# An adaLN block on one core: modulation rows folded in DRAM, half of the third block reloaded, and a new order of the last products

## The chip, the cores and the metric

The kernel runs on one core of one Trainium2 chip. The metric is the time of the whole execution on the device in microseconds (us), the median of several runs. The numbers of the profile come from one execution that was recorded by the hardware profiler; its own time stands beside the span in the table below.

## The reference, cut to what matters

```python
mod = (silu(c) @ w_mod).reshape(1, 6, 1, -1)            # c: 1 x 512, w_mod: 512 x 3072
sa, ca, ga, sb, cb, gb = (mod[:, i] for i in range(6))
h = layernorm(x) * (1 + ca) + sa                          # x: 2048 x 512
x = x + ga * linear_attention(h, wqkv, wo)                # 32 heads of 16
h = layernorm(x) * (1 + cb) + sb
x = x + gb * (mish(h @ w1 + b1) @ w2)                     # 512 -> 1792 -> 512
```

Everything is float32.

## The kernel before, in words

**Blocks and precision.** The 2048 rows are four blocks of 512 rows, numbered 0 to 3. Each float32 operand of a matmul is split into an upper part (ScalarE, a copy to `fp32r`) and a lower part (VectorE, a subtraction); a product is then three matmuls, upper by upper, upper by lower, lower by upper.

**The modulation.** `w_mod` lies transposed in DRAM (`wmodt`, 3072 x 512), and `load_wmod(i)` (L165) brings 128 of its rows into the tile `wm_i`. `mod_col(i, ...)` (L247) multiplies the tile by silu(c) and sums along the row on VectorE, which gives one column of `mc`, the table of modulation columns. Tiles 0 to 11 are plain rows. Tiles 12 to 23 (shift, scale and gate of the second half of the network) need their rows in another order, in which the 512 features are cut into pieces of 32, so `load_wmod` makes four DMAs of 32 rows each for one tile (L171, L172). All of them are issued on SP's queue. `mod_side` (L537) loads a tile and multiplies it three ticks later; tiles 20 to 23 and 16 to 19 are handled beside the query products of blocks 0 and 1 (from `beside_q`, L1026), tiles 12 to 15 beside the query product of block 2. A tick is one call of `tick()` (L121), which lets every running side job take one step; the order of instructions on each engine is thus fixed by the program's text. A product of w1's rows in the same other order is already folded by a copy from DRAM to DRAM, `fold_rows` (L806), in the loop over blocks at b == 1.

**Attention.** After the query products stand, for each block, the division by the attention's denominator (`attend`, L901: rows of 1/den are written to DRAM, read back broadcast as the tiles `rd`, and VectorE multiplies them into `q` on L925), the split into `qs` and the output product `o_unit` (L947), whose twelve matmuls per 128 rows use `qs_0` to `qs_3` in turn.

**The MLP.** Both GEMMs of the MLP use the Strassen scheme in Winograd's form: two blocks of rows are taken together, and seven products m1 to m7 replace eight. The first GEMM runs as `pair(L, g)` (L1510) for L = 0 (blocks 0, 1) and L = 2 (blocks 2, 3) and g = 0 to 6. The second GEMM consists of units (L1577), each one product for one g and both halves of 128 columns; `units` (L1869) lists them in order. For L = 2 the order is m1, m2, m4, m5, m6, m7, m3, and every product is a run of 42 matmuls of 512 columns over g = 6, 0, 1, ... 5 (`ORDER`, L1574). m6 and m7 add onto the accumulator of m1 (`pa`), m3 in effect onto m5, m2 has `pb`, m4 has `pd`, m5 has `pc`. The accumulators `pa`, `pb`, `pc` take two PSUM banks of the four with the tag `acc`; for L = 2, m4 takes banks with the tag `h`. The left operand of a unit is made by `left_job` (L1473): sums of activations for m5, m6 and m3 on VectorE (L1484, L1480, L1490 to L1493), then the split, upper part on ScalarE (L1283), lower part on VectorE (L1289). The right operand is loaded by `right_job` (L1456) from sums of w2 that were stored in DRAM (`w2d`, `w2t`).

**How results leave.** With L = 2 the left half of block 2 comes from m1 and m2. `result_job` (L1630) gates it on VectorE (L1636), transposes it (L1647) and adds it into the block's residual `x1d[2]` in DRAM by an accumulating DMA on POOL's queue (L1657). The right half of block 2 is two parts: one from m5 and m6 by the same path, one from m3. m3 is computed last and the other way round, four groups t of 128 rows of 21 short matmuls (L1930 on); its end (`ends`, L1938) multiplies by the gate and adds onto `rows_t`, whole rows of block 2 that were reloaded from `x1d[2]` after both sums had landed (L1909 to L1913). `put` (L1944) writes the whole rows to the output. Block 3 is added on chip: its residual is loaded as `rq` (L1603), `rows_half` (L1661) gates, transposes and adds m7's and m5's results in four pieces (c = 0, 1 by i = 0, 1), and after the last of them four DMAs write the block with pieces of 128 columns (L1684 to L1688). Blocks 0 and 1 are copied from `x1d` to the output inside DRAM by `copy_out` (L1716), a job that is added when the first unit of m4 of L = 2 comes up (L1901).

**Who sets the order.** From the MLP on, the order of instructions comes from a planner that runs when the kernel is built (`drive`, L1229; `best_job`, L1164): jobs carry a due time, and a model of costs in the table `T` (L27) decides which step of which job each engine's queue gets next. DMAs marked ANY go to POOL's or SP's queue, whichever the model has free; eight DMAs may be outstanding per queue (`lanes`, L1130). Each engine executes its queue in order, so an instruction that waits holds all that stand behind it.

## Time and profile before

| what | number |
|---|---|
| time, median of 3 runs | 485.88 us (485.56 to 488.79) |
| time of the profiled execution | 486.17 us |
| its span, first to last instruction | 484.4 us |
| TensorE (PE) busy | 97% of the span |
| VectorE (DVE), ScalarE (ACT), GpSimd (POOL) busy | 86%, 66%, 33% |
| mean granted TensorE clock | 0.993 |

The page and the views divide the span by engine. A row of the timeline gives start, duration, engine, line, operation, output<-inputs and shape; what stands in brackets is the idle time of the engine before it, and what ended that. PEld is TensorE's weight load, SPq, ACTq and POOLq are the queues that issue DMAs. In the table by windows, a number in brackets counts instructions, and the last three columns are the granted TensorE clock, the mean busy share of the sixteen DMA engines, and GB/s. In the table of DMA queues a row has packets, MB and the time that the packets took as a share of sixteen engines' time.

### The profile page before, as it was taken

The page shows a single profiled execution, that of the slowest core. Times are in us where ns is not written, and L with a number is a line of the kernel's source. Part 1 is how long each engine was busy: PE and PEld are TensorE (multiplying, and loading weights), DVE is VectorE, ACT ScalarE, POOL GpSimd, SP SyncE. Part 2 cuts the span into 40 slices and gives each one's busy share as a digit, 9 for nine tenths or more (in the row PEclk, how much of TensorE's full clock was granted, in tenths as well). Part 3 has the DMA queues.
Part 4 walks back from the last instruction along what each step waited for, and adds up shares of the span by engine and source line. Part 5 has one row for each costly group of instructions (what it writes and reads, how often), then busy time and mean ns, then how long its engine had stood idle before and what let it go on. Part 6 is the DMA issues. An engine that isn't in the chain of part 4 may idle for free.

```text
span 484.4 us, 7380 instructions
## 1 busy us (share of the span) xinstructions
PE 471.9 (97%) x2300; PEld 386.0 (80%) x2300; DVE 418.2 (86%) x818; ACT 322.0 (66%) x583; POOL 159.7 (33%) x239
## 2 busy tenths in 40 slices
PE   8999999999998999999999999999999999999993
PEld 6788887877886888888888888877888888888793
DVE  6989999899779878999987899989986587989892
ACT  6777686865543888779988998577567548627310
POOL 4583320000012413136543132542132243833250
PEclk9999999999998999999999999999999999999998
DMA  8953699143598456469999675986253389999977
GB/s 311 401 201 89 179 166 263 33 142 101 166 239 201 143 146 202 175 200 352 390 285 300 211 227 163 266 299 213 71 162 91 100 211 267 226 333 278 234 98 239
DMA packets 73776, 101.43 MB, mean 209 GB/s; under 512 B 24001, under 2 KB 46025, under 8 KB 73706
## 3 DMA queue, kind: packets, MB, share of 16 engines
q1 hardware_dynamic: 48104, 55.99, 36.8%
q0 software_dynamic: 24144, 43.67, 35.8%
q10 hardware_dynamic: 1490, 1.31, 0.9%
q8 instruction: 18, 0.29, 0.3%
q14 instruction: 20, 0.16, 0.1%
HBM read 69.48 MB, written 35.13 MB: 216 GB/s over the span
## 4 chain that ended last, share of the span: by engine, by line
PE 80%; DMA 6%; DVE 5%; SPq 3%; ACT 2%; issue 2%; POOL 0%; ACTq 0%; DVEq 0%
PE p_a L1506 18%; PE pa L1591 12%; PE p_s L1506 7%; PE pc L1591 6%; PE pb L1591 4%; PE o L140 3%; PE o L138 3%; PE o L139 3%; PE pq_a L475 3%; PE pd L1591 3%; DMA wm<-in_wmodt_dram 2%; SPq L333 2%; PE pk L140 2%; PE pk L138 2%; PE pk L139 2%
## 5 line engine op out<-in xcount | busy, mean ns | idle before, releaser
L1521 ACT ACTIVATE u<-p_a 128x512 f32<-128x512 f32 x42 | 24.9, 595 | 25.3 <-PE p_a L1506 23.5
L1530 ACT ACTIVATE u_a<-c_a,b1c 128x512 f32<-128x512 f32 x42 | 30.3, 722 | 16.2 <-DVE c_a L1527 14.0
L1527 DVE TENSOR_TENSOR c_a<-p_s,u 128x512 f32<-128x512 f32 x28 | 19.3, 688 | 15.7 <-PE p_s L1506 9.4
L1657 POOL DMA_DIRECT2D x1d<-turned x20 | 22.1, 1743 | 29.2 <-DVE turned L1647 29.2
L1465 POOL DMA_DIRECT2D wt_m<-w2t x25 | 20.0, 1216 | 30.0 <-PE pc L1591 8.2
L1465 POOL DMA_DIRECT2D wt_m<-w2d x17 | 13.3, 1035 | 18.6 <-DVE s_5l L1289 5.5
L1480 DVE TENSOR_TENSOR u_a<-u_a,u_a 128x512 f32<-128x512 f32 x28 | 18.1, 687 | 0.0
L913 POOL DMA_DIRECT2D rden_d<-rden x2 | 1.4, 715 | 50.3 <-DVE rden L911 50.3
L938 POOL DMA_DIRECT2D x1d<-r x16 | 9.0, 564 | 24.1 <-DVE r L942 16.8
L273 POOL TENSOR_TENSOR rs_n<-rs_n,half 128x1 f32<-128x1 f32 x16 | 11.2, 704 | 15.1 <-DVE rs_n L299 8.9
L366 ACT ACTIVATE e_k<-pk 128x512 f32<-128x512 f32 x15 | 8.9, 592 | 10.7 <-PE pk L140 10.6
L1625 ACT ACTIVATE U<-pa,mc 128x512 f32<-128x512 f32 x10 | 6.9, 687 | 11.4 <-PE pa L1591 11.2
L249 DVE SCALAR_TENSOR_TENSOR wm<-wm,sc_row 128x512 f32<-128x512 f32 x16 | 10.6, 679 | 3.4 <-DMA wm<-in_wmodt_dram 3.4
L1307 POOL DMA_DIRECT2D w1p<-w1d x12 | 9.2, 766 | 12.6 <-ACT u_a L1530 3.0
L369 DVE SCALAR_TENSOR_TENSOR ku<-e_k,relu_k 128x512 f32<-128x512 f32 x15 | 10.7, 714 | 2.9 <-ACT relu_k L367 2.9
L273 POOL TENSOR_TENSOR rs_x<-rs_x,half 128x1 f32<-128x1 f32 (+1 forms) x10 | 7.8, 781 | 16.0 <-DVE rs_x L268 14.6
L925 DVE SCALAR_TENSOR_TENSOR q<-q,rd 128x512 f32<-128x512 f32 x16 | 10.5, 687 | 2.9 <-DMA rd<-rden_d 2.9
L369 DVE SCALAR_TENSOR_TENSOR q<-e_q,relu_q 128x512 f32<-128x512 f32 x16 | 10.7, 687 | 2.6 <-ACT relu_q L367 2.6
L378 POOL DMA_DIRECT2D ku<-ku x8 | 7.1, 890 | 16.5 <-DVE ku L369 16.5
L1527 DVE TENSOR_TENSOR c_a<-p_a,u 128x512 f32<-128x512 f32 x14 | 9.6, 686 | 2.9 <-PE p_a L1506 2.2
L1558 ACT ACTIVATE u_a<-p_a,b1c 128x512 f32<-128x512 f32 x14 | 9.6, 684 | 3.0 <-PE p_a L1506 2.8
L1289 DVE TENSOR_TENSOR l_m_6l<-u_a,l_m_6h 128x512 fp32r<-128x512 f32 x12 | 8.2, 688 | 1.9 <-ACT l_m_6h L1283 1.8
(1505 smaller groups left out, 1889.3 us busy)
## 6 DMA issues: line engine op xcount, KB each, us to landing
wt_m<-w2t SPq DMA_DIRECT2D x27, 256.0 KB, 9.0
wt_m<-w2t POOLq DMA_DIRECT2D x25, 256.0 KB, 6.4
wt_m<-w2d POOLq DMA_DIRECT2D x17, 256.0 KB, 9.2
r<-in_x_dram SPq DMA_DIRECT2D x16, 256.0 KB, 2.7
x1d<-r POOLq DMA_DIRECT2D x16, 256.0 KB, 4.2
x<-in_x_dram SPq DMA_DIRECT2D x15, 256.0 KB, 5.4
w2d<-b SPq DMA_DIRECT2D x15, 256.0 KB, 8.2
w1d<-in_w_dram SPq DMA_DIRECT2D x4, 896.0 KB, 6.2
```

Of the source, the lines that this page charges most:

```text
L138: pe.matmul(o, st[0], mv[0], start=start, stop=False)
L139: pe.matmul(o, st[0], mv[1], start=False, stop=False)
L140: pe.matmul(o, st[1], mv[0], start=False, stop=stop)
L273: pool.tensor_tensor(y, y, half[:, lo:hi], op=ALU.pow)
L369: dve.scalar_tensor_tensor(dst, e, 1.0, r, op0=ALU.min, op1=ALU.add)
L1465: q.dma_start(f32(v), (w2d if src == "w2d" else w2t)[g][:, :, part, :])
L1506: pe.matmul(p, st, mv, start=onto is None and c == 0 and i == 0, stop=c == 1 and i == 2, skip_group_check=onto is not None)
L1521: act.activation(t["u", n], t["pa"], AF.Copy)
L1527: dve.tensor_tensor(t[key], t[p], t["u", n], op=ALU.add)
L1530: act.activation(u, t[key], AF.Mish, bias=b1c[:, f:f + 1])
L1591: pe.matmul(o, st[:, cs], mv, start=not onto and n == 0 and k == 0, stop=n == G - 1 and k == 2, skip_group_check=onto)
L1657: q.dma_start(rows_, sq, accum_op=ALU.add)
```

## The change

Five things are done together. (1) Twelve DMAs copy the second half of `wmodt` inside DRAM into `wmd`, already in the other order, right after w1's last fold; tiles 12 to 23 then load with one DMA each. (2) The second GEMM of L = 2 runs its products in the order m1, m2, m5, m6, m4, m7, m3. (3) Of block 2 only the right half is reloaded (`rows_t` is 128 x 4 x 64) and written at the end; the left half is copied from `x1d[2]` to the output inside DRAM, once its sum has landed. (4) Block 3 leaves in two sets of four DMAs, left halves of the strips after c = 0, right halves after c = 1, and gather, turn and addition of one piece are one step of the planner. (5) For four of the seven g of m3 the lower parts are subtracted on POOL instead of VectorE. Besides, due times and costs in `T` change, for the planner to use.

```diff
- 'early_at': -1.0,
+ 'early_at': -1.3,
- 'squares_due': 96.5,
- 'turn_due': 88.0,
+ 'squares_due': 89.9,
+ 'turn_due': 82.3,
- 'left_early': 16.4,
+ 'left_early': 17.4,
- 'copy_due': 10.8,
- 'result_due': 3.8,
+ 'copy_due': 12.9,
+ 'result_due': 3.7,
- 'out01': 48.2,
+ 'out01': 53.7,
- 'add': 0.8}
+ 'by_pool': 4,
+ 'left_out': 10.0,
+ 'add': 0.1}
...
+    wmd = drp.tile([3 * D, 512], F32, name="wmd")
+    def fold_mod(n, c):
+        sp.dma_start(wmd[D * n:D * (n + 1), :].rearrange("(x c r) f -> c r x f", c=4, r=32)[c],
+                     wmodt[D * (n + 3):D * (n + 4), :].rearrange("(c x r) f -> c r x f", c=4, r=32)[c])
     def load_wmod(i):
         wm[i] = sb(f"wm_{i}")
-        if i < 12:
-            sp.dma_start(wm[i], wmodt[P * i:P * (i + 1), :])
-        else:
-            r0 = 512 * (i // 4) + 32 * (i % 4)
-            for c in range(4):
-                sp.dma_start(wm[i][32 * c:32 * (c + 1), :], wmodt[r0 + P * c:r0 + P * c + 32, :])
+        src, r0 = (wmodt, P * i) if i < 12 else (wmd, P * (i - 12))
+        sp.dma_start(wm[i], src[r0:r0 + P, :])
...
             if b == 1:
                 fold_rows(t, sp)
+                if t == 3:
+                    for n in 2, 1, 0:
+                        for c in range(4):
+                            fold_mod(n, c)
...
+    BY_POOL = (2, 3, 4, 5)[4 - T['by_pool']:]
...
     def split_steps(...):
-            dve.tensor_tensor(lo, t, f32(hi), op=ALU.subtract)
+            (pool if lower_on == POOL else dve).tensor_tensor(lo, t, f32(hi), op=ALU.subtract)
...
-        yield d_(lower, n, makes=makes)
+        yield step_(POOL, 1.4, lower, makes=makes) if lower_on == POOL else d_(lower, n, makes=makes)
...
     def rows_half(...):
+        def chain():
+            gather()
+            turn_()
+            dve.tensor_tensor(v(), v(), t3(q[1]), op=ALU.add)
-        yield d_(gather, needs=[] if keep else [("T4", L)])
-        yield d_(turn_)
-        yield d_(lambda: dve.tensor_tensor(v(), v(), t3(q[1]), op=ALU.add), needs=[("rq", L, 1)], makes=[("v", c, i)])
-        for n in range(4) if c and i else ():
+        yield d_(chain, 1600, needs=[("rq", L, 1)] + ([] if keep else [("T4", L)]), makes=[("v", c, i)])
+        for n in range(4) if i else ():
             def put(queue, n=n):
-                sq, rows_ = strip_squares(rq[L, 1], out_rows(L + 1), n)
+                sq, rows_ = strip_squares(rq[L, 1], out_rows(L + 1), n, 64 * c, 64 * (c + 1))
                 queue.dma_start(rows_, sq)
...
-    units += [(L, name, g) for name in ("m1", "m2", "m4", "m5", "m6", "m7") for g in ORDER[L]]
+    units += [(L, name, g) for name in ("m1", "m2", "m5", "m6", "m4", "m7") for g in ORDER[L]]
...
             if l == L and (name, g) == ("m6", ORDER[L][0]):
                 add_job(load_r(L, 1), now[0] + T['r_due'])
+                add_job(iter([dma_(lambda q: q.dma_start(left_half(out_rows(L)), left_half(x1d[L])),
+                                   (), [("sum", L, 0, 0)])]), now[0] + T['left_out'])
             if l == L and (name, g) == ("m7", ORDER[L][0]):
                 def rows_in(q, i):
-                    rows01.append(sb(f"rows_{i}"))
-                    q.dma_start(rows01[i], x1d[L][P * i:P * (i + 1), :])
-                add_job(iter([dma_(lambda q, i=i: rows_in(q, i), [("rows", i)], [("sum", L, 0, 0), ("sum", L, 0, 1)])
+                    rows01.append(sb(f"rows_{i}", F32, (P, 4, 64)))
+                    q.dma_start(rows01[i], right_half(x1d[L])[P * i:P * (i + 1)])
+                add_job(iter([dma_(lambda q, i=i: rows_in(q, i), [("rows", i)], [("sum", L, 0, 1)], size=LATE / 2)
...
-                            q.dma_start(out[512 * L + P * t:512 * L + P * (t + 1), :], rows01[t])
+                            q.dma_start(right_half(out_rows(L))[P * t:P * (t + 1)], rows01[t])
```

`left_half(d)` and `right_half(d)` take columns 0 to 63 and 64 to 127 of each of the four strips of 128 columns of a row, pieces of 64 float32 numbers, 256 bytes.

More of the change, by code (lines that the diff above doesn't have):

```diff
@@ L1274, in drive, with split_steps @@
             run_job(*best_job())
-    def split_steps(name, get, keep, key, makes, needs=(), n=512, then=None):
+    def split_steps(name, get, keep, key, makes, needs=(), n=512, then=None, lower_on=DVE):
         st = []
@@ L1496, in left_job @@
         yield from split_steps(f"l_{L}_{name}_{g}", lambda: s1s[L, g] if v is None else get(v), left, (L, name, g),
-                               [("l", L, name, g)], needs)
+                               [("l", L, name, g)], needs, lower_on=POOL if L and name == "m3" and g in BY_POOL else DVE)
     def product(L, g, lft, rgt, tag="h", onto=None):
@@ L1678, in rows_half @@
         t3 = lambda t: t.rearrange("q (m s) -> q m s", s=32)
+        def chain():
+            gather()
+            turn_()
+            dve.tensor_tensor(v(), v(), t3(q[1]), op=ALU.add)
         if keep:
             yield a_(kept, makes=[("U3", L, i)])
-        yield d_(gather, needs=[] if keep else [("T4", L)])
-        yield d_(turn_)
-        yield d_(lambda: dve.tensor_tensor(v(), v(), t3(q[1]), op=ALU.add), needs=[("rq", L, 1)], makes=[("v", c, i)])
-        for n in range(4) if c and i else ():
+        yield d_(chain, 1600, needs=[("rq", L, 1)] + ([] if keep else [("T4", L)]), makes=[("v", c, i)])
+        for n in range(4) if i else ():
             def put(queue, n=n):
-                sq, rows_ = strip_squares(rq[L, 1], out_rows(L + 1), n)
+                sq, rows_ = strip_squares(rq[L, 1], out_rows(L + 1), n, 64 * c, 64 * (c + 1))
                 queue.dma_start(rows_, sq)
-            yield dma_(put, (), [("v", a, b) for a in range(2) for b in range(2)], queue=(SP, ACT)[n % 2])
+            yield dma_(put, (), [("v", c, 0), ("v", c, 1)], queue=(SP, ACT)[n % 2])
     U2, U3 = {}, {}
@@ L1717, in copy_out, with left_half, right_half @@
         q.dma_start(out_rows(b), x1d[b])
+    def left_half(d):
+        return d.rearrange("n (c s) -> n c s", c=4)[:, :, 0:64]
+    def right_half(d):
+        return d.rearrange("n (c s) -> n c s", c=4)[:, :, 64:P]
     def norm_job(b, t):
@@ L1938, in ends @@
                         def ends():
-                            v = nat(rows01[t], 1)
+                            v = rows01[t].rearrange("p c (x r) -> p x c r", r=32)
                             q = sb(f"q_last_{t}", F32, (P, H))
```

## The prediction

> **What bounds the kernel now.** I read the page first, then TensorE's rows for places where it stands still.
>
> ```profile
> span 484.4 us, 7380 instructions
> PE 471.9 (97%) x2300; PEld 386.0 (80%) x2300; DVE 418.2 (86%) x818; ACT 322.0 (66%) x583; POOL 159.7 (33%) x239
> ```
>
> PE is the bound, and the change takes no matmul away. So time can come from two places only: gaps of PE inside the span, and the stretch after PE's last matmul. The windows around the one large gap:
>
> ```profile
> 149.00:153.00 4.00, 2.37 (x8) 0.99 (x7) 4.00 (x9) 2.39 (x6) 2.14 (x4) 1.00 0.67 192
> 153.00:157.00 4.00, 3.95 (x10) 3.17 (x11) 4.00 (x9) 0.91 (x2) 0.75 (x2) 0.57 1.01 217
> ...
> 150.23 0.40 PE L140 MATMUL o<-m_1h,qs_1l 128*128 128x512 f32 x1
> 151.29 0.50 PE L138 MATMUL o<-m_2h,qs_2h 128*128 128x512 f32 x1 [0.66 <-ACT qs_2h L146]
> 153.05 0.79 PE L140 MATMUL o<-m_2h,qs_2l 128*128 128x512 f32 x1 [1.02 <-DVE qs_2l L152]
> ```
>
> PE is busy 2.37 of 4 us while VectorE is busy all 4. Three products start between 150.23 and 153.05, one of them between the last two rows; at the 0.227 us of a run of 42 in 9.52 us (quoted below) they take 0.68, so 2.1 us are lost. In the next 4 us the granted clock is 0.57, which loses 4 x 0.43 = 1.7 us. Together 3.8 us. Why is VectorE late?
>
> ```profile
> 138.35 0.69 DVE L249 SCALAR_TENSOR_TENSOR wm<-wm,sc_row 128x512 f32<-128x512 f32 x1
> 142.49 0.69 DVE L249 SCALAR_TENSOR_TENSOR wm<-wm,sc_row 128x512 f32<-128x512 f32 x1 [3.44 <-DMA wm<-in_wmodt_dram]
> 143.30 1.29 DVE L925 SCALAR_TENSOR_TENSOR q<-q,rd 128x512 f32<-128x512 f32 x2
> 149.89 1.29 DVE L925 SCALAR_TENSOR_TENSOR q<-q,rd 128x512 f32<-128x512 f32 x2
> 152.31 0.69 DVE L152 TENSOR_TENSOR qs_2l<-q,qs_2h 128x512 fp32r<-128x512 f32 x1
> ```
>
> It stood 3.44 us before a modulation tile; from there to `qs_2l` it works through its list without a pause. That tile was late on SP's queue:
>
> ```profile
> wm<-in_wmodt_dram SPq DMA_DIRECT2D x48, 64.0 KB, 3.2
> 133.00 3.20 SPq L172 DMA_DIRECT2D wm<-in_wmodt_dram  x7
> ```
>
> Seven pieces cost the queue 3.20 us, 0.46 each; one 256 KB tile is four of them.
>
> The end:
>
> ```profile
> 428.17 9.52 PE pd L1591 x42
> 456.09 0.70 ACT U L1625
> 456.83 9.82 PE pa L1591 x42
> 476.60 0.13 PE m L140
> 477.21 0.42 DVE rows L1942
> ...
> 470.02 2.23 POOL L1911 DMA_DIRECT2D rows<-x1d  x4 [3.48 <-DMA x1d<-turned]
> 476.21 0.43 DVE L1942 TENSOR_TENSOR rows<-rows,q_last 128x256 f32<-128x256 f32 x1 [1.44 <-DMA rows<-x1d]
> 468.17 0.75 DVE L1671 SCALAR_TENSOR_TENSOR q<-pa,mc,T 128x512 f32<-128x512 f32 x1
> 471.99 0.89 SPq L1687 DMA_DIRECT2D out_dram<-rq  x2
> 474.46 3.56 SPq L1945 DMA_DIRECT2D out_dram<-rows  x2
> ```
>
> PE ends at 476.7, the last addition at 477.6, the last store is issued by 478.0, and the span ends at 484.4: 7.7 us after PE, 6.4 after the issue. The queues by window show why:
>
> ```profile
> DMA  9999999999999999999999996653211100000000
> ...
> q1 hardware_dynamic: 601, 0.30, 52.4%
> q10 hardware_dynamic: 590, 0.29, 51.9%
> ```
>
> The first line is 476 to 484.4 in slices of 0.21 us: the DMA engines are full until 481.0, done by 482.7, and the wrap-up takes the last 1.7. The other two are 475.5 to 477.5, almost only 512-byte pieces of block 3: 1.043 x 16 x 2 us / 1191 = 28.0 ns a piece. The reload of `rows` and the stores of block 3 and block 2 all come within these ten microseconds.
>
> **The change part by part.**
>
> *Modulation loads.* 48 pieces become 12 DMAs, so SP is free of 36 x 0.46 = 16 us of issuing. Even if a slot of SBUF holds the tile in question until the 133.00 of the row above, its only DMA is out 0.5 us later instead of three pieces after that, 1.4 us of the 3.44 at the least; the queue's 16 us make the whole of it likely. Behind the wait the next source is `rd`:
>
> ```profile
> 134.37 1.82 POOL L917 DMA_DIRECT2D rd<-rden_d  x3 [2.74 <-PE pq L140]
> DMA to landing us min/median/max: 4.9/7.2/8.2
> ```
>
> The first lands at 134.4 + 4.9 = 139.3 at the earliest, and VectorE would ask at 143.30 - 3.44 = 139.9; the second may cost up to about 1 us. `qs_2l` then ends at 153.0 - 3.4 = 149.6 to 150.6. PE wants it three products after 150.23, at 150.9. So the gap closes, narrowly, and with it the slow clock: gain 3.8. Bounds: 0 if `rd` takes the wait's place whole, 3.8 above.
>
> *The twelve folds.* 3.1 MB inside DRAM, issued after w1's.
>
> ```profile
> w1d<-in_w_dram SPq DMA_DIRECT2D x4, 896.0 KB, 6.2
> SPq L176 <- DVE ku L369: 16.5, 1, 16.5
> 30.00:60.00 30.00, 30.00 (x150) 25.09 (x150) 26.81 (x54) 20.77 (x34) 15.24 (x23) 1.00 0.43 114
> ```
>
> Four folds of 896 KB, 3.7 MB, land in about 6 us each, overlapping; I take 8 to 12 us for the twelve. SP has 16.5 us of nothing to do right behind them and the DMA engines are at 0.43, so I cost them at 0. Without that cover the next load of wq would wait, and what is late next is `q_left`, with 40 us to go: still 0. Bounds 0 to 1.
>
> *Order of products.* m6 comes 9.5 us earlier, m4 goes between m6 and m7. The wait of m7 for U2 (456.09 to 456.83) goes: 0.3 gained. But m5 now follows m2 directly, and its two `acc` banks are m2's own, which VectorE has to gather first:
>
> ```profile
> 427.53 0.75 DVE L1636 SCALAR_TENSOR_TENSOR q<-pb,mc,U 128x512 f32<-128x512 f32 x1 [1.99 <-PE pb L1591]
> ```
>
> The first bank is free at 428.3, PE wants it at 428.17; the second is free at 429.0, or 429.6 if another subtraction stands between. Cost 0.1 to 1.4, and I take 0.4, near the low end, since PE fills the first half for 0.7 us before it needs the second. Net +0.1. The sums for m5 and m6 are needed 9.5 us earlier, m4's splits later; VectorE's 1.99 us of idle in that row says that it has room. If it has not, each us late is one us of PE, and `qs`-like waits may lower the clock again.
>
> *Block 2 in halves, sum 9.5 us earlier.* The reload of `rows` can start some 9 us before 470.02, so the 1.44 us wait at 476.21 goes, with 512 KB of loading out of the last ten us. The copy of the left half and those of blocks 0 and 1 (moved with m4) fall into the stretch of m4 and m7; I cost them at 0 behind those 19 us of matmuls, and up to 1.5 if m3's tiles queue behind them.
>
> *Four subtractions on POOL, one chain.* VectorE's gather for m7's second half starts at 468.17, though PE wrote it by 466.65: subtractions for m3 stood before it. Four of them leave, at 0.69 each. They do not come free:
>
> ```profile
> 13.66 1.30 POOL L152 TENSOR_TENSOR wk_2l<-wr,wk_2h 128x512 fp32r<-128x512 f32 x1
> 14.42 1.08 DVE L658 TENSOR_TENSOR hT_x_1l<-hf_x,hT_x_1h 128x512 fp32r<-128x512 f32 x1
> 18.84 0.68 DVE L658 TENSOR_TENSOR hT_x_3l<-hf_x,hT_x_3h 128x512 fp32r<-128x512 f32 x1
> ```
>
> One takes POOL 1.30, and a subtraction of VectorE beside POOL takes 1.08 and not 0.68. So the relief is 4 x (0.69 - 0.40) = 1.2 us. The left half of block 3 can be issued near 468.9 (gather from 466.9, turn, addition), its pieces move from about 470.8, the right half two us later.
>
> *The stores.* Block 3 is now 4096 pieces of 256 bytes, block 2's half 2048. No plain store of that size is in the trace. The nearest rows:
>
> ```profile
> q1 hardware_dynamic: 7311, 0.91, 50.0%
> q0 software_dynamic: 2123, 0.55, 90.8%
> y_x<-xd SPq DMA_DIRECT2D x16, 64.0 KB, 2.8
> ```
>
> The first is 60 to 72 us, plain 128-byte pieces: 0.5 x 16 x 12 us / 7311 = 13.1 ns. The second is 462 to 470 us, accumulating pieces of 256 bytes: 54.7 ns. On the line from 13.1 (128) to 28.0 (512), 256 bytes take 18 ns. I take 18, as plain pieces resemble plain ones: 6144 x 18 / 16 = 6.9 us from 470.8, done by 477.7, before the last store is issued. Then that store is alone: issue from 477.67, 2.8 us to land as the loads of the third row, 1.7 of wrap-up: 482.2 in place of 484.4. Gain 2.2; bounds -9.1 (54.7 ns) and 2.8.
>
> *Due times in T.* They change the planner's order only, from the MLP on.
>
> ```profile
> 157.00:445.00 288.00, 287.93 (x1336) 236.81 (x1336) 251.67 (x480) 212.58 (x386) 105.22 (x156) 1.00 0.76 220
> ```
>
> From 157 to 445 us PE is never idle, so there is nothing to gain there; the 36 us of VectorE's idle time in this row are the cover, and I cost the edits at 0. Where the cover fails, a late operand is a wait of PE; I allow up to 1.5.
>
> Sum on the profiled execution: 486.17 - 3.8 - 2.2 + 0.1 = 480.3. That execution is 0.3 above the median of the runs, so the forecast is 480.0 us.
>
> **The rivals.**
>
> *Small pieces cost as much as 512-byte ones.* At 28.0 ns the stores take 10.8 us and end at 481.6; the tail gives 1.1 and not 2.2: 481.1. For it: in the same window a piece of 512 bytes costs barely more than twice one of 128. Against it: the line through both.
>
> *Slower: each 256-byte piece is read and written back.* The place is the last 15 us. At 54.7 ns, 6144 pieces take 21.0 us from 470.8, the span ends at 493.5, and the time is 480.0 + 2.2 + 9.1 = 491.3. It decides from about 41 ns a piece, where it eats the front's gain. Against it: only accumulating pieces show that price. The Trainium skill, "DMA: Bandwidth & Descriptors", Specifications, speaks for it: transfers below 512 bytes make the DMA engine read, modify and write. The 128-byte pieces at 13.1 ns, all loads, do not bear that out; no run here shows it for stores.
>
> *The front's gap stays in part.* If `rd` or a full VectorE list makes PE wait 1 us or more there, the clock may fall again, and 1.9 to 3.8 us come back: about 483. For it: the margin above is 0.3 to 1.3 us.
>
> *A new wait near the end.* The four POOL subtractions (5.2 us) stand in POOL's queue with the reload of `rows`, whose wait for the sum was 3.48 us; m3 needs them from 467.4 on. Or m5 waits long for its banks. Price 2.5: 482.5.
>
> **How the numbers follow.** Forecast 0.51, 512-byte price 0.18, gap stays 0.13, new wait 0.12, slower 0.06. A measurement of this kernel can tell about 1%, that is 481.0 and 490.7. Below 481.0 lies most of the forecast (0.45), nearly half of the first rival and a little of the others: 0.56. Above 490.7: the slow rival and a corner of a bad planner order, 0.07. Within: 0.37. The range goes from 478.2 (all upper bounds) to 484.5 (gap and tail each half missed); only the slow rival and a sum of two bad cases lie outside.
>
> **What would show it.** Right: no wait of VectorE on `wm` near 140, clock 1.00 from 149 to 157, about 12 SP issues of 256 KB for tiles 12 to 23; PE's last matmul some 3.7 us earlier; under 6 us from there to the end; 256-byte pieces near 18 ns. Wrong: DMA engines full until the end, a wait of m5 over 1 us at m2's end, a wait of m3 on POOL, or any PE gap between 157 and 445.

## The result, and the profile after

The kernel after takes 481.53 us (median of 4 runs, 480.9 to 482.57), the kernel before 486.82 in the same comparison (4 runs, 485.56 to 488.79): a ratio of 0.9897, 95% interval 0.9863 to 0.9932. The profiled execution took 481.15 us, 5.0 less than the one of before. In a second comparison, with more runs of before, the ratio was 0.9868 (0.9831 to 0.9905). The page's head:

```profile
span 479.4 us, 7305 instructions
PE 469.4 (98%) x2300; PEld 385.0 (80%) x2300; DVE 419.7 (88%) x814; ACT 322.1 (67%) x583; POOL 164.1 (34%) x241
```

The 5.0 us can be laid out along TensorE (PE), which does the same 2300 matmuls in both kernels. The first row of each pair below is of before, the second of after (timeline, start and duration in us); the rows are the first matmul of the MLP.

```profile
202.65 0.39 PE L1506 MATMUL p_a<-b_0h,a_0h 128*128 128x512 f32 x1
```

```profile
198.63 0.39 PE L1515 MATMUL p_a<-b_0h,a_0h 128*128 128x512 f32 x1
```

So 4.0 us are won before the MLP. From there to the last block's m1 the kernel after takes 0.8 longer (207.1 against 206.3), for m1 to m7 0.6 longer (58.15 against 57.52), and from the last matmul to the end 2.4 less (5.6 against 8.0). -4.0 + 0.8 + 0.6 - 2.4 = -5.0.

**The front, after.** The DMA issues (count, KB each, median us to landing):

```profile
wmd<-in_wmodt_dram SPq DMA_DIRECT2D x12, 256.0 KB, 7.6
wm<-wmd SPq DMA_DIRECT2D x12, 256.0 KB, 6.0
```

VectorE's products with the modulation tiles among the groups (busy us, mean ns of one, idle us ahead of them), and then its only wait between 136 and 150 (us in total, times, longest):

```profile
L253 DVE SCALAR_TENSOR_TENSOR wm<-wm,sc_row 128x512 f32<-128x512 f32 x16 | 10.5, 675 | 0.0
```

```profile
DVE q L933 <- DMA rd<-rden_d: 1.3, 1, 1.3
```

The two windows in which the gap lay:

```profile
149.00:153.00 4.00, 3.83 (x17) 2.86 (x16) 4.00 (x11) 2.50 (x6) 2.09 (x4) 1.00 0.79 220
153.00:157.00 4.00, 4.00 (x46) 3.00 (x45) 4.00 (x9) 1.48 (x3) 0.97 (x2) 1.00 0.18 44
```

VectorE no longer waits for a `wm` tile (idle 0.0 in that group), and waits 1.3 for `rd` instead. PE is busy 3.83 of 4 us where it was 2.37, and the granted clock of the next window is 1.00 where it was 0.57.

**The middle, after.** A wait that before did not have, in the timeline on PE, behind it on VectorE, and the store behind both on POOL:

```profile
312.11 0.50 PE L1600 MATMUL pd<-l_m_4h,t_4l 128*128 128x512 f32 x1 [1.34 <-DVE t_4l L1298]
...
311.36 0.69 DVE L1298 TENSOR_TENSOR t_4l<-t,t_4h 128x512 fp32r<-128x512 f32 x1 [1.69 <-DMA w2t<-t_3h]
...
304.64 0.55 POOL L1456 DMA_DIRECT2D w2t<-t_3h  x1 [0.25 <-ACT t_3h L1292]
```

`t_4l` is to be written where `t_3h` still lies; the store of `t_3h` was issued at 304.64 and had not landed.

**The last products, after.** The timeline of PE where m5 (`pc`) follows m2 (`pb`), and two rows of the chain that ended last, VectorE's second gather of m2 and the product behind m5:

```profile
424.54 0.39 PE L1600 MATMUL pb<-l_m_5h,wt_m 128*128 128x512 f32 x1
425.14 0.47 PE L1600 MATMUL pc<-l_m_6h,wt_m 128*128 128x512 f32 x1 [0.21 <-issue]
...
425.67 0.40 PE L1600 MATMUL pc<-l_m_6h,wt_m 128*128 128x512 f32 x1
426.35 0.50 PE L1600 MATMUL pc<-l_m_6h,wt_m 128*128 128x512 f32 x1 [0.28 <-DVE q L1645]
...
425.55 0.76 DVE q L1645
...
435.48 9.52 PE pa L1600 x42
```

In each pair the starts lie 0.60 and 0.68 us apart, where a run has 0.23. So m5 waited twice, 0.37 and 0.45 us, until VectorE had read m2's banks (the gather at 425.55 is the second). The profile puts the first wait down to `issue`; the kernel with m5 in other banks, below, shows that both were for banks. Behind them the products follow each other without a gap.

**The end, after.** The timeline of VectorE, with the first piece of block 3 (gather, transpose, addition) and the second addition, and of GpSimd (POOL) beside it:

```profile
459.32 0.75 DVE L1680 SCALAR_TENSOR_TENSOR q<-pa,mc,T 128x512 f32<-128x512 f32 x1 [1.62 <-PE pa L1600]
460.11 0.71 DVE L1684 STREAM_TRANSPOSE t<-q 128x512 f32<-128x512 f32 x1
460.85 3.37 DVE L1691 TENSOR_TENSOR rq<-rq,t 128x512 f32<-128x512 f32 x1
465.66 0.69 DVE L1691 TENSOR_TENSOR rq<-rq,t 128x512 f32<-128x512 f32 x1
...
460.75 1.67 POOL L1298 TENSOR_TENSOR l_m_4l<-u_a,l_m_4h 128x512 fp32r<-128x512 f32 x1
462.01 1.66 POOL L1298 TENSOR_TENSOR l_m_5l<-u_a,l_m_5h 128x512 fp32r<-128x512 f32 x1
```

The DMA engines from 470 to 479.4 (40 slices of 0.235 us, then packets, MB and share per queue):

```profile
DMA  9988799998999999999999998589999721000000
DMA packets 5979, 1.48 MB, mean 158 GB/s; under 512 B 5979, under 2 KB 5979, under 8 KB 5979
q10 hardware_dynamic: 3097, 0.77, 42.9%
q1 hardware_dynamic: 2882, 0.71, 37.8%
```

The same addition takes 3.37 us beside GpSimd's subtractions and 0.69 without them. The DMA engines are full to 477.4, 3.6 us behind the start of the last matmul; nearly all packets are pieces of 256 bytes (the mean is 248), and one costs 0.807 x 16 x 9.4 us / 5979 = 20.3 ns.

### The profile page after: what moved, and what is told of

The parts are those of the page before. It is cut to its first block, busy times and chain, and to the rows that moved or that the text cites. A ratio compares the mean times of both kernels' runs of the same rounds, so it can differ in the third digit from the quotient of the medians.

```text
span 479.4 us, 7305 instructions
## 1 busy us (share of the span) xinstructions
PE 469.4 (98%) x2300; PEld 385.0 (80%) x2300; DVE 419.7 (88%) x814; ACT 322.1 (67%) x583; POOL 164.1 (34%) x241
## 4 chain that ended last, share of the span: by engine, by line
PE 80%; DVE 9%; DMA 4%; issue 2%; SPq 2%; ACT 1%; POOL 1%; ACTq 0%; DVEq 0%; POOLq 0%
PE p_a L1515 18%; PE pa L1600 12%; PE p_s L1515 7%; PE pc L1600 6%; PE pb L1600 4%; PE o L142 3%; PE o L140 3%; PE o L141 3%; PE pq_a L479 3%; PE pd L1600 3%; PE pk L142 2%; SPq L337 2%; PE pk L140 2%; PE pk L141 2%; PE gacc L141 1%
## 5 line engine op out<-in xcount | busy, mean ns | idle before, releaser
L1474 POOL DMA_DIRECT2D wt_m<-w2t x29 | 24.1, 1179 | 43.4 <-PE pa L1600 16.8
L1292 ACT ACTIVATE l_m_6h<-u_a 128x512 fp32r<-128x512 f32 x12 | 7.4, 621 | 6.1 <-DVE u_a L1489 6.1
```

The costliest lines, as they stand in the source:

```text
L1474: q.dma_start(f32(v), (w2d if src == "w2d" else w2t)[g][:, :, part, :])
```

## The experiments

In the table, "front" is the start of the MLP's first matmul, "middle" from there to the last block's m1, "products" from m1 to m3, and "tail" from the start of the last matmul to the end of the span, all in us of the one profiled execution. The time is the median; the ratio is to the kernel before, run in turns on the same chip (its median was 488.18 beside the fold alone, the kernel without it, the subtractions on VectorE and the old order; 488.31 beside after again, the old due times and the two kernels with whole stores and rows; 487.23 beside the last four of the table). Runs of before are far apart (484.7 to 490.1), so a ratio is less sharp than the kernel's own runs. The tail repeats better: five executions share the order, the stores and the place of the subtractions (after twice, without fold, old due times, old `add`), and their tails lie between 5.6 and 5.9.

| kernel | time | ratio, 95% interval | front | middle | products | tail |
|---|---|---|---|---|---|---|
| before | 486.82 | 1 | 202.65 | 206.3 | 57.5 | 8.0 |
| after | 481.53 | 0.9897 (0.9863 to 0.9932) | 198.63 | 207.1 | 58.15 | 5.6 |
| after, again | 481.33 | 0.9868 (0.9831 to 0.9905) | 200.32 | 206.5 | 58.2 | 5.8 |
| fold alone | 483.40 | 0.9898 (0.9875 to 0.9920) | 199.40 | 206.2 | 57.5 | 9.0 |
| without fold | 485.99 | 0.9962 (0.9939 to 0.9986) | 203.96 | 208.2 | 58.2 | 5.7 |
| subtractions on VectorE | 480.62 | 0.9843 (0.9819 to 0.9867) | 199.89 | 206.8 | 58.2 | 4.7 |
| old order | 483.53 | 0.9890 (0.9861 to 0.9919) | 199.14 | 206.8 | 59.0 | 7.3 |
| old due times | 481.02 | 0.9858 (0.9820 to 0.9896) | 200.62 | 206.65 | 58.2 | 5.8 |
| block 3 stored whole | 483.01 | 0.9898 (0.9859 to 0.9938) | 199.54 | 206.5 | 58.2 | 7.8 |
| whole rows of block 2 | 482.89 | 0.9900 (0.9864 to 0.9935) | 198.00 | 206.9 | 58.2 | 6.8 |
| VectorE and banks | 479.64 | 0.9851 (0.9830 to 0.9872) | 198.95 | 206.4 | 57.1 | 4.7 |
| old `add` | 482.19 | 0.9898 (0.9882 to 0.9913) | 199.91 | 206.6 | 58.2 | 5.9 |
| VectorE, banks, old `add` | 479.78 | 0.9850 (0.9827 to 0.9873) | 199.23 | 206.8 | 57.1 | 5.0 |
| old order, VectorE | 481.93 | 0.9890 (0.9871 to 0.9908) | 198.36 | 209.4 | 57.55 | 5.7 |

The theory at the outset: the fold closes the front's gap and that is most of the gain; the tail's gain is made by the early sums and the earlier stores, less what GpSimd's subtractions cost. The rival: the parts depend on each other, or other edits (due times, order) made the gain.

### The fold alone

Before, with `wmd`, `fold_mod` and the new `load_wmod`, and nothing else.

> The kernel before with one part of the change: the twelve folding transfers in DRAM and the single loads of 256 KB for the last twelve modulation tiles. Nothing else is changed. Theory (the fold alone closes the front gap): TensorE's first qkv product group ends about 3.7 us earlier, VectorE waits for no `wm` near 140, the clock granted in 149 to 157 is 1.00, and the time is the time of before less 3.3 to 4.1, so about 482.4 profiled against 486.17. Rival (the front gap closed because of the other due times, or the gain in the front is given back in the planned middle): 484.5 to 486.2.

Measured: 483.40 against 488.18, 4.8 less by the medians. The profiled 483.77 lies between the two expectations (about 482.4, and 484.5 or more). The front comes 3.25 earlier in the one profile. In the windows there the clock stays at 1.00 as in after, while PE is busy for 3.07 us of the first and not for 3.83:

```profile
149.00:153.00 4.00, 3.07 (x14) 2.15 (x13) 4.00 (x9) 3.24 (x7) 2.48 (x5) 1.00 0.71 180
153.00:157.00 4.00, 4.00 (x46) 3.05 (x45) 4.00 (x10) 0.71 (x2) 0.07 (x1) 1.00 0.37 84
```

The waits:

```profile
PE o L140 <- DVE qs_2l L152: 0.9, 1, 0.9
DVE q L931 <- DMA rd<-rden_d: 2.0, 2, 1.2
```

The fold is the cause of the gain in the front. It is not complete: VectorE now waits 2.0 us for `rd`, and PE 0.9 for `qs_2l`, but the clock stays at 1.00. The tail, 9.0, gained nothing without the other parts; it was 1.0 longer than in the profile of before.

### After without the fold

```diff
...
-        src, r0 = (wmodt, P * i) if i < 12 else (wmd, P * (i - 12))
-        sp.dma_start(wm[i], src[r0:r0 + P, :])
+        if i < 12:
+            sp.dma_start(wm[i], wmodt[P * i:P * (i + 1), :])
+        else:
+            r0 = 512 * (i // 4) + 32 * (i % 4)
+            for c in range(4):
+                sp.dma_start(wm[i][32 * c:32 * (c + 1), :], wmodt[r0 + P * c:r0 + P * c + 32, :])
...
-                if t == 3:
-                    for n in 2, 1, 0:
-                        for c in range(4):
-                            fold_mod(n, c)
```

The tensor `wmd` and `fold_mod` are gone, too.

> The kernel after with the fold taken back alone: the twelve folding transfers are gone and the last twelve modulation tiles come by four pieces each again. Everything behind the front stays. Theory: the front gap is back (TensorE's wait at 149 to 153, granted clock under 0.8 in 153 to 157), the tail keeps its gain, and the time is 481.15 + 3.7 = 484.8 profiled, that is 1.3 us under before. Rival (the two parts are not independent: the gain in the tail hangs on the earlier arrival): 486 or more.

Measured: 485.99 against 488.18, 2.2 less by the medians, and a tail of 5.7 that kept its gain. By the time alone the rival's "486 or more" came true (the median is at its edge, the profiled execution took 487.75), but before itself was slower beside these runs (488.18), and the tail kept its gain without the fold. Against before the parts add up: 4.8 for the fold and 2.2 for the rest are the 7.0 of the second comparison of after (481.33 against 488.31). The first comparison gave 5.3, and each part is known only to 1.1 us either way, so a smaller dependence is not excluded. VectorE waited twice for `wm`, and PE stood still ahead of `gb_ps`, by the waits and by the windows:

```profile
DVE wm L251 <- DMA wm<-in_wmodt_dram: 6.3, 2, 3.5
PE gb_ps L531 <- DVE rden L912: 2.4, 1, 2.4
```

```profile
145.00:149.00 4.00, 1.65 (x9) 1.06 (x8) 3.57 (x8) 2.10 (x4) 0.00 (x0) 1.00 0.69 180
149.00:153.00 4.00, 3.56 (x16) 2.61 (x15) 4.00 (x8) 0.10 (x1) 0.69 (x1) 1.00 0.67 202
153.00:157.00 4.00, 2.30 (x10) 1.27 (x9) 4.00 (x10) 3.30 (x7) 2.88 (x5) 1.00 0.76 240
```

The expectation missed one thing: PE lost 2.35 + 0.44 + 1.70 us in these windows, and yet the clock stayed at 1.00.

### The four subtractions on VectorE

```diff
-    lower_on=POOL if L and name == "m3" and g in BY_POOL else DVE
+    lower_on=DVE
```

> The kernel after with the four subtractions of m3's left tiles on VectorE again instead of GpSimd; the planner places them. Theory (GpSimd's subtractions of 1.67 us lengthen VectorE's addition of `rq` beside them from 0.69 to 3.37 us, so moving them costs more than it relieves): VectorE's addition takes 0.69 us again, four subtractions of about 0.4 come back on VectorE (1.6 us), and the piece of block 3 that leaves first is issued 0 to 1 us earlier than at 468.52; the time is 480.3 to 481.2. Rival (the prediction's step: the relief of 1.2 us on VectorE is real, and without it the sums come later): left half issued 1 to 2 us later, time 482.0 to 483.0.

Measured: 480.62 (480.48 to 481.22). VectorE's addition is 0.69 again, behind m3's lower parts, which end at 461.1 on VectorE; the third row is SP's queue:

```profile
460.42 0.69 DVE L1298 TENSOR_TENSOR l_m_5l<-u_a,l_m_5h 128x512 fp32r<-128x512 f32 x1
462.55 0.69 DVE L1691 TENSOR_TENSOR rq<-rq,t 128x512 f32<-128x512 f32 x1
...
467.54 4.03 SPq L1699 DMA_DIRECT2D out_dram<-rq  x4
```

The left half of block 3 is issued at 467.54 and not 468.52, although PE was 1.0 us later in this execution: 2.0 us earlier against m3's start. The tail is 4.7 against 5.6 to 5.8. So the subtractions on GpSimd cost the tail about 1.0 us, and the rival, that they bring relief, is refuted. The other kernels bear it out: with the new order and both halvings the tail is 5.6 to 5.9 in the five executions with the subtractions on GpSimd and 4.7 to 5.0 in the three without (two of which use other banks as well). The DMA engines from 468 to 479.5 (slices of 0.29 us) show what was won:

```profile
DMA  1928998899999999999999999999421069400000
out_dram<-rows SPq DMA_DIRECT2D x2, 128.0 KB, 2.3
```

The engines are idle when the last store's pieces begin at 477.2, and the row stores of SP's queue land in 2.3 us by the median (4.8 in after).

### The old order of the products

```diff
-("m1", "m2", "m5", "m6", "m4", "m7")
+("m1", "m2", "m4", "m5", "m6", "m7")
```

> The kernel after with the last block's products in the order m1, m2, m4, m5, m6, m7 of before. Theory (the new order costs 0.6 us at m5's banks and pays for itself because m7, m6 and the sum of block 2 are not what sets the end): TensorE's two waits of 0.37 and 0.45 us after m2 go, a wait of about 0.3 before m7 comes back, m3 starts some 0.5 us earlier, and if the chain that ends the kernel hangs on TensorE the time is 480.5 to 481.0. Rival (the new order buys the early sums, so that the tail's transfers start earlier): the tail from TensorE's end to the end of the span grows by 1 to 2 us and the time is 482 to 483.

Measured: 483.53, and a tail of 7.3. The rows of block 2 hold up the end:

```profile
474.76 0.43 DVE L1962 TENSOR_TENSOR rows<-rows,q_last 128x256 f32<-128x256 f32 x1 [2.97 <-DMA rows<-x1d]
476.70 0.42 DVE L1962 TENSOR_TENSOR rows<-rows,q_last 128x256 f32<-128x256 f32 x1 [1.18 <-DMA rows<-x1d]
```

The new order buys some 1.6 us of tail here; the rival was right. The theory's 0.5 on PE did not come either: m7 waited 1.1 us for a `wt_m` tile, so the products took 59.0.

### Old order, subtractions on VectorE

Both edits above. It asks whether the order or GpSimd's queue, in which the subtractions stood between the accumulating stores of block 2, made the rows late.

> The kernel after with the products in the old order m1, m2, m4, m5, m6, m7 and the four subtractions on VectorE. With the old order alone the rows of block 2 came late: the queue of GpSimd carried its subtractions between the accumulating stores of block 2, and the tail grew from 5.6 to 7.25. Theory (the order itself buys the early sum): the tail stays over 6.2 us, rows land after 475, time 1 to 2 over the kernel with the subtractions on VectorE and the new order (480.6). Rival (GpSimd's queue held the sums back, and the order is worth nothing without it): tail 4.6 to 5.2, time within 0.4 of that kernel, or 0.6 under it because the waits at the third product go.

Measured: a tail of 5.7, between the two expectations, products of 57.55. The rows still make VectorE wait 2.06 us. So of the 1.6 some 0.6 was GpSimd's queue, and 1.0 is the order's own (5.7 against 4.7). The order costs 0.6 of PE (58.15 against 57.55) and pays 1.0; from the start of m1 to the end of the span the new order takes 72.8 and the old one 73.4, so it is worth about half a microsecond net. The time, 1.3 over the kernel with the new order, cannot be split further: this execution's middle lost 2.6 us to a longer wait for `t_4l`, and the runs came from two chips.

### Six due times of before

```diff
- 'early_at': -1.3,
+ 'early_at': -1.0,
...
- 'squares_due': 89.9,
- 'turn_due': 82.3,
+ 'squares_due': 96.5,
+ 'turn_due': 88.0,
...
- 'left_early': 17.4,
+ 'left_early': 16.4,
...
- 'copy_due': 12.9,
- 'result_due': 3.7,
+ 'copy_due': 10.8,
+ 'result_due': 3.8,
```

> The kernel after with six due times of before (early_at, squares_due, turn_due, left_early, copy_due, result_due); out01, add and everything else stay as after. Theory (the wait of 1.34 us for `t_4l` near 311 comes from the order in which the planner places transfers with the new due times, so that the slot of `t_3h` comes free late): the wait is under 0.6 us, the middle (first `p_a` to the last block's m1) takes 206.2 to 206.5 instead of 207.1, and the time falls by 0.5 to 0.9 against the kernel after. Rival (the wait comes from the earlier arrival that the fold brings, or from `add`): the wait stays over 1.0 and the time is within 0.4 of the kernel after. A third outcome that the fold alone points at: the first `p_a` comes 0.8 later, as there (199.40 against 198.63), and takes back what the middle gains.

Measured: 481.02 against 481.33 of after beside it, the wait for `t_4l` 0.9. The wait lies between the two expectations (under 0.6, over 1.0), and inside what the unchanged kernel showed in its two profiles (1.34 and 0.6). The time fits the rival: these six due times are worth nothing that can be seen, and the wait in the middle is not theirs. The seventh, `out01`, was not tried alone.

### The old `add`

```diff
- 'add': 0.1}
+ 'add': 0.8}
```

The instructions of the engines up to 430 us are those of after but for the place of one ScalarE instruction, and with it the slots of a few tiles.

> The kernel after with the planner's charge `add` (for GpSimd's accumulating stores) at 0.8 again instead of 0.1. Near 311 this moves one ScalarE instruction (`a_1h`, issued between the two `t_4h`) behind both, and moves the tiles' slots with it. Theory (`add` sets the order, the order hands `t_4l` the slot whose store is still under way, and that is the wait of 0.8 to 1.5 us): the wait at 311 is gone or under 0.4, the middle takes 206.1 to 206.4 us instead of 206.5 to 207.1, and the time falls by 0.3 to 0.8 if the tail, whose order the charge changes too, stays as it is. Rival (the wait comes from the transfers' speed there): a wait of 0.8 or more stays.

Measured: the wait is gone, PE is full from 308 to 312 (window), VectorE writes `t_4l` without waiting (timeline), and PE's one wait from 300 to 330 is another (the last row):

```profile
308.00:312.00 4.00, 4.00 (x19) 3.31 (x18) 4.00 (x11) 1.63 (x3) 1.61 (x3) 1.00 1.10 386
...
310.86 0.68 DVE L1298 TENSOR_TENSOR t_4l<-t,t_4h 128x512 fp32r<-128x512 f32 x1
...
PE p_a L1515 <- ACT u L1530: 0.3, 1, 0.3
```

So `add`, through the order of one ScalarE instruction and the slots that follow from it, made that wait. But that other one, 0.33 near 327, is new against after (before lost 0.07 near 330), the middle is 206.6, a little over the 206.4 that was expected at most, and the median is 482.19: nothing is gained. In all kernels with 0.1 the same wait was there, 0.6 to 2.1 us long.

### Block 3 stored whole

```diff
-        for n in range(4) if i else ():
+        for n in range(4) if c and i else ():
...
-                sq, rows_ = strip_squares(rq[L, 1], out_rows(L + 1), n, 64 * c, 64 * (c + 1))
+                sq, rows_ = strip_squares(rq[L, 1], out_rows(L + 1), n)
...
```

The stores then wait for all four pieces of the block.

> The kernel after with block 3 stored in one set of four transfers of 512-byte pieces behind the last piece, as before, instead of two sets of 256-byte pieces. Theory (a 256-byte piece costs 20 ns and a 512-byte piece 28 to 30, so the two sets cost 5.1 us of the sixteen DMA engines' time against 3.7, but 2.1 us of it starts earlier): the engines idle near 469 to 471, the stores end together 0 to 1.0 us later, time plus 0 to 0.8. Rival (the first half's early start is worth its whole lead of 2.1 us): time plus 1.5 to 2.1. Rival (the pieces are dear and the two sets are a loss): time 0.3 to 1.0 lower.

Measured: 483.01 against 481.33, tail 7.8: plus 1.7 and plus 2.0. The DMA engines from 468 to 481.9 (slices of 0.35 us), and the window of 473 to 474, which holds 512-byte pieces alone:

```profile
DMA  6589940000089999999899999999999997100000
...
DMA packets 349, 0.18 MB, mean 179 GB/s; under 512 B 0, under 2 KB 349, under 8 KB 349
q10 hardware_dynamic: 175, 0.09, 48.9%
```

The engines idle from 470.1 to 471.8, and then a 512-byte piece costs 0.97 x 16 x 1 us / 349 = 44.5 ns and not the 28.0 of before (0.97 is the row's share and the 48.1% of the other queue). From 472 to 477 the mean is 41.2 (1893 packets, 97.4%). The first rival was right by its size, for a reason that it did not name: 2048 x 41.2 and 4096 x 20.3 ns are nearly the same work (5.3 and 5.2 us of sixteen engines), so the small pieces cost nothing and the head start counts whole.

### Whole rows of block 2

```diff
...
-                    rows01.append(sb(f"rows_{i}", F32, (P, 4, 64)))
-                    q.dma_start(rows01[i], right_half(x1d[L])[P * i:P * (i + 1)])
+                    rows01.append(sb(f"rows_{i}"))
+                    q.dma_start(rows01[i], x1d[L][P * i:P * (i + 1), :])
...
-                            q.dma_start(right_half(out_rows(L))[P * t:P * (t + 1)], rows01[t])
+                            q.dma_start(out[512 * L + P * t:512 * L + P * (t + 1), :], rows01[t])
```

The copy of the left half is gone, too, and the reload waits for both sums of block 2.

> The kernel after with block 2's rows reloaded and stored whole, as before, and without the left half's copy in DRAM. Theory (the tail is bound by the DMA engines from 469.5 on, and the whole rows put 256 KB more into it by 2048-byte pieces, 128 more microseconds of single-engine time or more, while the right halves' 256-byte pieces cost about the same as whole rows): rows land 1 to 2 us later, the last store is issued 0.5 to 1.5 later, time plus 0.5 to 1.5. Rival (the halving is neutral, the order of the products and the two sets bought the tail): within 0.3.

Measured: 482.89 against 481.33, tail 6.8, plus 1.6 and plus 1.0. The runs lie far apart (481.11 to 485.28), so the tail is the surer of the two. The size is as expected, its place is not: the rows were reloaded in time, and no addition waited. The last store left 1.2 us after the start of the last matmul, as in after, but with twice the bytes. The 128 us of single-engine time in the expectation are shown by no run: all packets from 468 to the end of this kernel, block 3's among them, took 0.731 x 16 x 11.8 = 138 us.

### Subtractions on VectorE, m5 in other banks

```diff
-    lower_on=POOL if L and name == "m3" and g in BY_POOL else DVE
+    lower_on=DVE
...
-        tag = "h" if L and name == "m4" else "acc"
+        tag = "h" if L and name == "m5" else "acc"
...
-            add_job(kept_job(L, "pd", 0, "T4", T4, [("T4", L)], ["h" if L else "acc"]), soon)
+            add_job(kept_job(L, "pd", 0, "T4", T4, [("T4", L)], ["acc"]), soon)
...
-                        last[t] = ps("h" if t < 3 else "tp", f"m3_{t}")
+                        last[t] = ps(("h", "acc", "acc", "tp")[t], f"m3_{t}")
...
```

> The kernel after with the four subtractions on VectorE and with m5 in the two `h` banks, m4 in two `acc` banks, and the last product's four results in one `h`, two `acc` and the `tp` bank. Theory (the two waits of 0.37 and 0.45 us before the third product are waits for m1's or m2's banks, and without GpSimd's subtractions the end hangs on TensorE's last matmul, 4.67 us before the end): both waits go, the last block's six products take 57.4 to 57.6 us instead of 58.15, and the time is 0.4 to 0.9 under the kernel with the subtractions on VectorE alone, about 480.0. Rival (the end hangs on the DMA engines, full from 468 to 477): TensorE ends earlier and the tail grows by as much, same time as there within 0.3.

Measured: 479.64 (478.82 to 480.9). The chain has all products back to back, and the DMA engines from 468 to 477.1 (slices of 0.23 us) run nearly empty before the last store's pieces:

```profile
415.04 9.52 PE pb L1600 x42
424.56 9.52 PE pc L1600 x42
434.08 9.52 PE pa L1600 x42
...
DMA  8999999899999999999999999995316990000000
```

The products take 57.1 and the tail is 4.7. The theory holds in the profile: both waits were waits for banks, and with the subtractions gone from GpSimd the end hangs on PE's last matmul again, so that PE's gain stays: the products are 1.0 shorter than with the subtractions on VectorE alone, and the tail is the same 4.7. In the times the new banks are not seen: the median is 1.0 lower, but on another chip, and the ratio to before is 0.9851 (0.9830 to 0.9872) against 0.9843. That the two edits together beat the kernel after is seen in the profile (products 1.0 and tail 0.9 to 1.1 shorter) and in the medians, 1.7 to 1.9 apart on different chips; the intervals of the ratios still overlap.

### All three

Subtractions on VectorE, m5 in other banks, `add` at 0.8.

> The kernel after with all three: the four subtractions on VectorE, m5 in the `h` banks, and `add` at 0.8. Theory (three separate costs of about 0.9, 0.6 and 0.5 us): 479.3 to 480.2 in the median, a ratio of 0.980 to 0.985 to the kernel before, faster than both kernels of the change. Rival (with the smaller `add` gone, the last sums and reloads are planned later and the tail grows): 480.5 to 481.5.

Measured: 479.78 (477.77 to 480.95), as the kernel without the third edit. The time is in the theory's range, but of its three costs the 0.5 of `add` did not come. PE has two small waits in the middle, 0.45 near 312 and 0.29 near 327, both for ScalarE's `u` and not for `t_4l`: in these runs `add` has no value of its own, it only chooses which operand comes late.

### After, again

> The kernel after, unchanged, beside the other three, so that they can be compared with it and not only with the kernel before. Expected: a ratio of 0.986 to 0.993 to before, and once more the account of the first profile: front 3.3 to 4.1 earlier, a wait of about 1.3 for `t_4l` near 311, two waits of 0.37 and 0.45 before the third product of the last block, an addition of `rq` of over 3 us beside GpSimd's subtractions, and 5 to 6 us from TensorE's last matmul to the end.

Measured: 0.9868, and the account as expected but for the front: its first matmul of the MLP came at 200.32, 1.7 later than in the first profile, with PE's wait for `qs_2l` at 1.0, and the wait for `t_4l` was 0.6. In the twelve executions with the fold the front lies between 198.0 and 200.6, so one profile places it only to about a microsecond and a half.

## Why the prediction was right, and where it was not

It gave 480.0 us and a range of 478.2 to 484.5; the time was 481.5. Of the 1.5 between them 0.9 lies in the kernel before, which stood at 485.88 by the three runs that the forecast started from and at 486.82 in the comparison. The gain was 5.3 by the medians of the first comparison and 7.0 by those of the second, and the forecast 5.9. The ends of its range do not follow from what it names for them: all upper bounds (3.8, 2.8 and 0.2) lead from 485.9 to 479.1, and half of the gap and half of the tail to 483.0; the measured time lies inside these, too. By its own steps:

**Modulation loads: right.** Gain 3.8 predicted, with bounds 0 and 3.8. Measured: 4.0 in the two first profiles, 3.25 for the fold alone in one profile, 4.8 in the medians (3.9 to 6.1 by the interval of the ratio); the front lies at 198.0 to 200.6 in the twelve executions with the fold and at 202.65 and 203.96 in the two without. `rd` did become the next source of VectorE's wait (0.6 to 2.7 us), and PE still loses up to 1.5 us there. The rival "the gap stays in part" had this right, but not its price: the clock stayed at 1.00 in every kernel with the fold, so that the wait itself is all it costs. The 1.7 us for the slow clock were true of the profile that they were read from: in the kernel after without the fold PE lost 4.5 us there at a clock of 1.00.

**The twelve folds: right.** They land in 7.6 us each (median), and PE came no later for them: its `gb_ps`, ahead of the gap, starts at 145.62 against 145.95.

**Order of products: mechanism right, cost mis-sized.** The wait of m7 for U2 went (0.3). The bank wait of m5 was taken at 0.4 and measured 0.37 + 0.45 = 0.82, since PE waited for each of the two banks. The net was +0.6, not +0.1. With other banks it goes (57.1 us).

**Block 2 in halves: right.** The wait of 1.44 for `rows` is gone, and whole rows cost 1.0 to 1.6 more. The prediction gave the earlier sum no price apart from that wait; between the two orders, both with the subtractions on VectorE, it is worth 1.0 of tail.

**Four subtractions on GpSimd: wrong, and it is the step that failed.** It said "So the relief is 4 x (0.69 - 0.40) = 1.2 us" and took as the price of contention a subtraction of 1.08 in place of 0.68. The price was an addition of 3.37 in place of 0.69, and the step costs 1.0 us instead of bringing 1.2. The row of 1.08 was VectorE beside one GpSimd subtraction; here three of the four stand back to back (459.50 to 463.67), and VectorE's addition, begun at 460.85, ends at 464.22, 0.55 us behind the last of them. The Trainium skill, "SBUF — State Buffer", Who interferes with whom, says that a VectorE instruction with two SBUF inputs contends with a GpSimd instruction that reads SBUF, and that one with at most one SBUF input, outside the 2-port modes, does not. The trace agrees: the addition has two, the gather (one input from PSUM) at 459.32 and the transpose at 460.11 kept their 0.75 and 0.71 beside the same GpSimd work.

**The stores: price right, tail right by two errors.** 18 ns a piece predicted, 20.3 measured; the bounds of 28.0 and 54.7 were far. (The prediction says that 28.0 and 13.1 ns come from the same window; they come from 475.5 to 477.5 and from 60 to 72.) Thus the two rivals on the price fall. The Trainium skill, "DMA: Bandwidth & Descriptors", Specifications, says that transfers below 512 bytes are read, modified and written; the plain 256-byte stores here show no price of that kind. The tail gained 2.4 against 2.2, but the nearness is luck. The last store was not alone, as the step had it: the engines were full to 477.4, because the left half left only at 468.52, 0.4 before the 468.9 of the forecast, although PE had begun m3 2.6 us earlier. With the subtractions on VectorE the last store is alone, and the tail is 4.7, 1.1 shorter than the 5.8 of the forecast (482.2 less 476.4): from that store's issue at 476.06 to the end of the span are 3.4 us, where the forecast has 4.5. So a store that was taken 1.1 too long stands against the 1.0 that GpSimd took.

**A new wait near the end: did not come.** PE has no wait behind the two of m5, which sum to less than the 1 us named as a sign of error.

**Due times: "nothing to gain" right, "0" wrong.** The prediction named any PE gap between 157 and 445 as a sign of error, and besides m5's waits, which it had priced, there is one of 1.34 us (0.6 in the second profile). It allowed up to 1.5 for it. The cause is the planner's charge `add`, not the due times.

**The sum.** Predicted -3.8 + 0.1 - 2.2 = -5.9; measured -4.0 + 0.6 - 2.4 + 0.8 = -5.0. The 0.9 between them is the order's 0.5 and the middle's 0.8, less what the front and the tail gave more. PE's last matmul came 2.6 us earlier, not 3.7, for the same two reasons.

## What to carry to other kernels

Before a piece of work is moved to an idle engine, look at what the busy engine runs beside it: GpSimd was 33% busy, but the work given to it stretched one VectorE addition to five times its length, ahead of the stores that ended the kernel. A run of small DMAs that releases one late tile is worth folding where a copy can run in idle time. And splitting a store into two halves pays when the first half can leave while the engines idle, provided that the smaller pieces move as many bytes per microsecond, which is to be read from packets and share in that stage and not from another.

## What the runs showed of the hardware

**A 512-byte store piece has no one price.** It was 28.0 ns in the kernel before, where the two queues carried almost only such pieces at 475.5 to 477.5. In the kernel that stores block 3 whole, also with almost only such pieces, it was 44.5 ns at 473 to 474 and 33.9 ns at 475 to 476 (493 packets, 104.5%). What differs was not found.

**The clock does not fall with every gap of one length.** The kernel with the old order and VectorE's subtractions, in two windows of the middle:

```profile
308.00:312.00 4.00, 2.49 (x11) 1.72 (x10) 1.59 (x5) 2.27 (x4) 0.94 (x2) 1.00 1.03 401
312.00:316.00 4.00, 3.45 (x8) 2.77 (x9) 4.00 (x10) 1.15 (x2) 1.36 (x4) 0.57 0.40 154
```

The row of the timeline that ends the gap:

```profile
312.55 0.79 PE L1600 MATMUL pd<-l_m_4h,t_4l 128*128 128x512 f32 x1 [2.06 <-DVE t_4l L1298]
```

A wait of 2.06 us, and the clock is 0.57 in the window behind it. Without the fold, PE waited 2.35 us near 146, and the clock stayed at 1.00. So a gap's own length is certain, and the clock behind it is a risk; whether the gap's place in time decides was not tried. It may be part of why the times of before spread so far: its runs lie between 484.7 and 490.1 at mean clocks of 0.997 to 0.988, those of the kernel with VectorE's subtractions between 480.5 and 481.2 at 0.998 to 1.0.
